# Dilated rows of four streams in one load, a fourth token group's products inside attention, and the next weights converted at its end

## The chip, the cores and the metric

The kernel runs on one core of a Trainium2 chip. The core has a matrix engine (TensorE, PE in the profile), a vector engine (VectorE, DVE), an activation engine (ScalarE, ACT), GpSimd (POOL) and SyncE (SP), which only issues transfers; 16 DMA engines move the data. The metric is the device time of one execution in microseconds, lower is better.

## The reference

Attention over q, k, v of shape (4 batches, 8 heads, 576 positions, 64) in float32, then two gated layers over the 2304 tokens:

```python
rel = pos[:, None] - pos[None, :]
mask_plain = (rel >= 0) & (rel < 32)                        # heads 0 to 3
mask_dil = (rel >= 0) & (rel < 128) & (rel % 4 == 0)        # heads 4 to 7
attn = softmax(where(mask, q @ k.T / 8, -1e9)) @ v
x = attn.transpose(0, 2, 1, 3).reshape(2304, 512)
x = (silu(x @ w_gate) * (x @ w_val)) @ w_out                # 512 -> 1536 -> 512
x = (((x @ w1) * (x @ w2)) @ w3) @ w_out2                   # 512 -> 1024 -> 1024 -> 512
```

The weights come as float64.

## The kernel before

**Attention** is worked through in 18 superblocks `u`, each of 128 query rows: 128 consecutive tokens for the plain heads ("near") and 64 rows of each of two residue streams for the dilated heads ("far"). A dilated head only sees positions of its own residue modulo 4, so each residue is a stream of 144 rows with a plain window of 32. A `part` is one batch and a pair of the four residues; the eight parts lie end to end, 64 rows to a superblock. A far row of a load is thus two streams wide: 128 floats, 512 bytes in one piece. A near row is 64 floats, 256 bytes. Tokens become complete in the order of the parts: the four residues of one batch need two parts, so tokens 0 to 511 are complete after superblock 4, not 3.

The schedule is written out by hand (`manual_schedule`): every engine executes its instructions in program order. The loop is `for u in range(-3, 20)`, and a turn of it is called step `u` here. In step `u` the program has, in this order: loads of q and k for `u+5` (`load_qk`), copies of the transposed probabilities of `u-1` (`t_p_out`), the result of `u-2` as a high part (`x_out_hi`, ScalarE), loads of v for `u+2` (`load_v`), exp of `u+1`, scores and the row maximum of `u+2` (`scores`, `softmax_a`), the low part of the result of `u-2` (`x_out_lo`, VectorE), transposes of q and k of `u+3` (`t_qk`), parts of weight conversions (`part_jobs`), the sums of `u+1` (`softmax_b`) and its division on POOL (`softmax_n`), then transposes of the probabilities of `u` (`t_p`) and the product with v of `u-1` (`av`). Scores are the first thing that PE does in a step, so the start of `sc` on PE marks steps. near and far tiles have three buffers, the v tiles four. SyncE issues all near loads, and the far loads of q and k from superblock 1 on; ScalarE issues the far loads of superblock 0, the far loads of v from superblock 1 on (`vfar`), and the first three weight loads, in halves.

**Weights.** A conversion job turns one 512 KB piece of float64 weights into a high and a low part: five VectorE operations (L115 to L125), a cast on ScalarE (L196), a subtraction on POOL (L197). `part_jobs` runs the jobs `early` (the slice c=0 of w_gate, w_val and w_out) in six parts each: one part a step in steps 1 to 6, two a step in steps 7 to 9, and the last job in steps 17 and 18.

**Filling.** `fill` puts single matmuls of the first layer's up-products (24 for a group of 512 tokens: 12 for the gate, 12 for the value) between attention's, at most four a step until step 15, more in steps 16 to 19. Three of the five token groups are worked off this way. Their results pass through PSUM banks `po3`, `pa` and `pb`; `pa` and `pb` have two buffers each, and attention uses them too. av of the last superblock uses the bank `po2`.

**After attention** PE goes over the slices c (12 of the first layer, 8 of the second) and the five groups: `up_mm`, `up_act`, then `down` of the step before; the products of `down` go through `po0` to `po3` and are added up by VectorE. Conversions of the next slice follow behind `down` (`next_job`).

Of the kernel before, what the change touches and what calls it, by code (L numbers as in the profile page):

```python
# [12 lines left out]
I32 = mybir.dt.int32  # L13
# [10 lines left out]
KW = QB + WINDOW  # L24
NIDLE = 8
SQ = 32
NEG = -1.0e9
# [6 lines left out]
def attention_ffn_kernel(  # L34
# [103 lines left out]

    def job_load_half(job, half):

        _, a, j = job
        if half == 0:
            raw_of[job] = wp.tile([P, 2 * PW], I32, tag="wraw", name=f"raw_w{a}_{j}", bufs=3)
        raw = raw_of[job]
        if j < 2:
            h = slice(half * KT // 2, (half + 1) * KT // 2)
            nc.scalar.dma_start(
                out=raw.rearrange("p (k f) -> p k f", f=2 * P)[:, h],
                in_=words((w_gate, w_val)[j])[:, a * 2 * P:(a + 1) * 2 * P].rearrange("(k p) f -> p k f", p=P)[:, h])
        else:  # L150
            h = slice(half * PW, (half + 1) * PW)
            nc.scalar.dma_start(out=raw[:, h], in_=words(w_out)[a * P:(a + 1) * P, h])

    def job_load(job):
# [46 lines left out]
    def jobs_of(c):  # L201

        res = [[] for _ in groups]
        if c + 1 < NCH:
            first = 1 if c else 2
            if c == NFT - 2:

                res[0].append(("w3", 0, 0))
                res[4].append(("w3", 0, 1))
            if c == NFT - 1:  # L210
                first = 0
            if NFT <= c:
                f = c + 1 - NFT
                res[0].append(("w3", f, 0))
                res[1].append(("w3", f, 1))
                first = 2
            for j in range(3 if c + 1 < NFT else 2):
                res[first + j].append(("w", c + 1, j))
        if 1 <= c <= NJ:
            res[4].append(("wo", c - 1, 0))  # L220
        return res

    early = [("w", c, j) for c in range(1) for j in range(3)]
    jobs += early
    for c in range(NCH):
# [26 lines left out]
    def part_jobs(u):  # L252

        n = len(early)
        for m, at in enumerate((-2, 1, 13)):
            if u in (at, at + 1):
                job_load_half(early[m], u - at)
                jpos[0] = m + 1
        third = PARTS // 3


        upto = max(0, min(u, third) + min(2 * max(u - third, 0), third) + max(0, min(third // 2 * (u - NU + 2), third)))
        while parts[0] < upto:
            next(running)
            parts[0] += 1


# [5 lines left out]


    starts = {}
    for part in range(NU * QB // RES):
        for u in range(NU):
            d = part * RES - u * QB
            if -WINDOW < d < QB:
                starts[u] = d  # L280

    MPER = NB if NB % 2 else NB // 2
    mask = []

    def build_masks():
        gen = att.tile([P, KW], F32, name="m_gen")
        nc.gpsimd.memset(gen, 0.0)
        for h in range(2):
            g = gen[h * QB:(h + 1) * QB, :]

            nc.gpsimd.affine_select(out=g, in_=g, compare_op=ALU.is_ge, fill=NEG,
                                    base=WINDOW, pattern=[[-1, KW]], channel_multiplier=1)
            nc.gpsimd.affine_select(out=g, in_=g, compare_op=ALU.is_ge, fill=NEG,
                                    base=-1, pattern=[[1, KW]], channel_multiplier=-1)
        for u in range(MPER):
            m = att.tile([P, 2, KW], F32, name=f"mask{u}")
            nc.vector.tensor_copy(out=m, in_=gen.rearrange("p (u c) -> p u c", u=1).to_broadcast([P, 2, KW]))
            for h in range(2):
                g = m[h * QB:(h + 1) * QB]
                if (2 * u + h) % NB == 0:  # L300
                    nc.gpsimd.memset(g[:, 0, 0:WINDOW], NEG)
                if u in starts:
                    d = starts[u]
                    if d <= 0:
                        nc.gpsimd.memset(g[:, 1, 0:WINDOW + d], NEG)
                    else:
# [4 lines left out]
            mask.append(m)  # L311

# [11 lines left out]
    RP = DIL // 2  # L324
    near_in, far_in, v_in = {}, {}, {}

    def stream(src, part):

        b, r = divmod(part, RP)
        return src[b, HH:H].rearrange("h (m r) d -> m h (r d)", r=DIL)[:, :, r * 2 * D:(r + 1) * 2 * D]  # L330

    def load_qk(u):
        near = att.tile([P, 2, HH, D], F32, tag="near", name=f"near{u}", bufs=3)
        far = att.tile([P, HH, 2 * D], F32, tag="far", name=f"far{u}", bufs=3)
# [10 lines left out]
        near_in[u], far_in[u] = near, far  # L345

    def load_v(u):
        near = att.tile([KW, 2, HH, D], F32, tag="vnear", name=f"vnear{u}", bufs=4)
        far = att.tile([KW, HH, 2 * D], F32, tag="vfar", name=f"vfar{u}", bufs=4)
# [7 lines left out]
        z = WINDOW if u == 0 else 0  # L357
        if z:
            nc.gpsimd.memset(far[0:z], 0.0)
# [4 lines left out]
        v_in[u] = near, far  # L364

    qkT = {}

    def t_qk(u):
# [5 lines left out]
        if u == 0:  # L374
            nc.vector.memset(kn[:, :, 0:WINDOW], 0.0)
            nc.vector.memset(kf[:, :, 0:WINDOW], 0.0)
        else:
            _, _, kn0, kf0 = qkT[u - 1]
            nc.scalar.copy(out=kn[:, :, 0:WINDOW], in_=kn0[:, :, P:])
            nc.scalar.copy(out=kf[:, :, 0:WINDOW], in_=kf0[:, :, QB:])  # L380
        t = near_in.pop(u)
# [37 lines left out]
    def softmax_a(u, par):  # L419
        if par == 0:  # L420
            sm[u] = att.tile([P, 2, NP, KW], F32, tag="s", name=f"s{u}", bufs=4)
            mx[u] = att.tile([P, 2, NP], F32, tag="mx", name=f"mx{u}", bufs=3)
        m = mask[u % MPER]
        s = sm[u][:, par]
# [44 lines left out]
    def av(u):  # L469
        near, far = v_in.pop(u)  # L470
        far = far.rearrange("k h (r d) -> k h r d", r=2)

# [14 lines left out]
    def x_parts(x, u):  # L487
# [3 lines left out]
        t = t[:, HP:NP, :].rearrange("d p (h q) -> d p h q", h=2)  # L491
        for row, cnt, part, m in runs(u * QB, QB, RES):
            b, r = divmod(part, RP)
            edge = min(max((CUT - b * S) // DIL - m, 0), cnt)
            for a, n in ((0, edge), (edge, cnt - edge)):
                if n:
                    xs = tokens(x, slice(HP, NP), b * S + DIL * (m + a), DIL * n)
                    yield (xs.rearrange("d p (m r) -> d p r m", r=DIL)[:, :, 2 * r:2 * r + 2, :],
                           t[:, :, :, row + a:row + a + n])

# [50 lines left out]
    def filling():  # L551
        for g in range(2):
            for j in range(2):

                pt = bank("po3", f"f{g}_{j}", 1) if (g, j) != (1, 1) else bank("pa", f"f{g}_{j}", 2)
                for n, _ in enumerate(up_product(0, g, j, pt)):
# [5 lines left out]
                    yield  # L562
        pa = bank("pa", "pa0_2", 2)
        pb = bank("pb", "pb0_2", 2)
        upp[0, 2] = pa, pb
        for j, pt in enumerate((pa, pb)):
            yield from up_product(0, 2, j, pt)

# [63 lines left out]
    for u in range(-3, NU + 2):  # L632

        filled[1] = sum(PER for b in range(3) if u > ((b + 1) * RP * RES - 1) // QB + 2)
        quota = 4 if u < NU - 2 else PER
# [6 lines left out]
        attention_end(u)  # L642
    assert filled[0] == 3 * PER

# [109 lines left out]
```

## Time and profile before

| | us |
|---|---|
| median of 3 runs | 892.32 (891.57 to 893.55) |
| the profiled execution | 893.95 |
| its span, first to last instruction | 892.1 |
| PE busy in the span | 868.4 (97%) |
| DVE, ACT, POOL busy | 596.6, 249.1, 305.9 |

The span is what the trace covers; 1.85 us of the profiled execution lie outside it. PE is busy nearly throughout, so what matters is where it stands idle, where it runs at its lower clock, and what it waits for there.

### The profile page before, as it was taken

How to read it: one execution, taken by the hardware profiler on the slowest of the kernel's cores; microseconds unless marked ns; L12 is line 12 of the kernel's file. 1: busy time of each engine (PE TensorE's matmuls, PEld its weight loads, DVE VectorE, ACT ScalarE, POOL GpSimd, SP SyncE). 2: the span in 40 equal slices, each digit the busy share in tenths (PEclk: the TensorE clock that was granted, in tenths of full speed). 3: DMA queues.
4: the chain of work that ended last, by engine and by line, in shares of the span. 5: the costliest groups of instructions: out<-in, count | busy, mean ns of one | idle time of the engine just before them, and what ended most of it. 6: DMA issues, size and time to landing. Idle time of an engine off the chain costs nothing.

```text
span 892.1 us, 13545 instructions
## 1 busy us (share of the span) xinstructions
PE 868.4 (97%) x5192; PEld 726.7 (81%) x5192; DVE 596.6 (67%) x1070; ACT 249.1 (28%) x514; POOL 305.9 (34%) x296
## 2 busy tenths in 40 slices
PE   6898999999999999999999999999999999999998
PEld 4677778888888888888888888888888888888886
DVE  5788766767667676676667784857575747575725
ACT  4778741222212222122221234222121212121211
POOL 5666523323223232232322358423231313231311
PEclk9899999999999999999999999999999999999999
DMA  9877611212112121121211220122121212120014
GB/s 188 187 164 167 155 48 48 70 49 72 48 48 72 48 71 48 48 71 48 71 48 48 71 62 10 41 55 52 43 59 37 63 45 60 47 68 27 1 48 165
DMA packets 113856, 61.77 MB, mean 69 GB/s; under 512 B 72320, under 2 KB 108800, under 8 KB 113792
## 3 DMA queue, kind: packets, MB, share of 16 engines
q1 hardware_dynamic: 104928, 55.73, 23.5%
q10 hardware_dynamic: 8864, 5.18, 2.3%
q8 instruction: 41, 0.67, 0.3%
q14 instruction: 23, 0.19, 0.1%
HBM read 56.16 MB, written 4.72 MB: 68 GB/s over the span
## 4 chain that ended last, share of the span: by engine, by line
PE 90%; DVE 4%; DMA 3%; SPq 1%; issue 0%; ACT 0%; POOL 0%; ACTq 0%; POOLq 0%
PE pa L525 27%; PE pb L525 27%; PE po L670 17%; PE po L690 11%; PE fold L704 5%; PE av L483 1%; DMA far<-in_k_dram 1%; PE pp L459 1%; PE sc L416 1%; PE f L525 1%; DMA vfar<-in_v_dram 1%; DVE x_lo L507 1%; DVE mx L431 1%; DMA vnear<-in_v_dram 1%; DVE s L425 1%; DVE mx L441 0%
## 5 line engine op out<-in xcount | busy, mean ns | idle before, releaser
L582 DVE TENSOR_TENSOR pr<-pb,ga 128x512 f32<-128x512 f32 (+1 forms) x98 | 62.5, 637 | 212.5 <-PE pb L525 108.4
L586 POOL TENSOR_TENSOR sl<-pr,sh 128x512 fp32r<-128x512 f32 (+1 forms) x100 | 118.5, 1185 | 232.7 <-ACT sh L585 232.7
L525 PE MATMUL pa<-x_hi,wlo 128*128 128x512 f32 (+1 forms) x392 | 143.4, 368 | 0.0
L525 PE MATMUL pa<-x_hi,whi 128*128 128x512 f32 (+1 forms) x392 | 143.3, 368 | 0.0
L525 PE MATMUL pb<-x_hi,whi 128*128 128x512 f32 (+1 forms) x392 | 143.3, 368 | 0.0
L525 PE MATMUL pb<-x_hi,wlo 128*128 128x512 f32 (+1 forms) x392 | 143.2, 367 | 0.0
L197 POOL TENSOR_TENSOR wlo<-val_w,whi 128x512 fp32r<-128x512 f32 x52 | 67.2, 1293 | 199.3 <-ACT whi L196 199.3
L656 DVE TENSOR_TENSOR y<-po,y 128x512 f32<-128x512 f32 (+1 forms) x220 | 131.3, 632 | 0.2 <-PE po L670 0.2
L525 PE MATMUL pa<-x_lo,whi 128*128 128x512 f32 (+1 forms) x392 | 128.5, 368 | 0.0
L525 PE MATMUL pb<-x_lo,whi 128*128 128x512 f32 (+1 forms) x392 | 128.4, 368 | 0.0
L585 ACT CAST sh<-pr 128x512 fp32r<-128x512 f32 (+1 forms) x100 | 57.9, 579 | 151.2 <-DVE pr L582 148.5
L196 ACT CAST whi<-val_w 128x512 fp32r<-128x512 f32 x52 | 32.3, 621 | 233.6 <-DVE val_w L125 233.6
L670 PE MATMUL po<-sh,wlo 128*128 128x512 f32 (+1 forms) x240 | 88.4, 368 | 0.6 <-POOL wlo L197 0.6
L670 PE MATMUL po<-sh,whi 128*128 128x512 f32 (+1 forms) x240 | 88.5, 369 | 0.4 <-ACT whi L196 0.4
L670 PE MATMUL po<-sl,whi 128*128 128x512 f32 (+1 forms) x240 | 88.4, 368 | 0.0
L525 PEld LDWEIGHTS pa<-x_hi,wlo 128*128 128x128 f32 x392 | 73.9, 188 | 12.8
L525 PEld LDWEIGHTS pa<-x_hi,whi 128*128 128x128 f32 x392 | 73.9, 188 | 12.7
L525 PEld LDWEIGHTS pb<-x_hi,whi 128*128 128x128 f32 x392 | 73.9, 189 | 12.2
L525 PEld LDWEIGHTS pb<-x_hi,wlo 128*128 128x128 f32 x392 | 73.9, 189 | 12.1
L525 PEld LDWEIGHTS pb<-x_lo,whi 128*128 128x128 f32 x392 | 72.5, 189 | 12.2
L525 PEld LDWEIGHTS pa<-x_lo,whi 128*128 128x128 f32 x392 | 72.4, 188 | 12.3
L656 DVE TENSOR_TENSOR o<-po,o 128x512 f32<-128x512 f32 x126 | 81.4, 685 | 0.2 <-PE po L690 0.2
(100 smaller groups left out, 1345.7 us busy)
## 6 DMA issues: line engine op xcount, KB each, us to landing
raw_w<-in_moe_w_dram SPq DMA_DIRECT2D x256, 32.0 KB, 1.8
raw_w<-in_moe_w_dram SPq DMA_DIRECT2D x16, 512.0 KB, 3.5
raw_w<-in_moe_w_gate_dram SPq DMA_DIRECT2D x11, 512.0 KB, 3.7
raw_w<-in_moe_w_val_dram SPq DMA_DIRECT2D x11, 512.0 KB, 3.6
raw_w<-in_moe_w_out_dram SPq DMA_DIRECT2D x11, 512.0 KB, 3.5
out_dram<-o SPq DMA_DIRECT2D x18, 256.0 KB, 2.1
raw_wo<-in_moe_w_out_dram SPq DMA_DIRECT2D x8, 512.0 KB, 3.4
vnear<-in_v_dram SPq DMA_DIRECT2D x32, 96.0 KB, 4.0
```

The lines of the kernel that those rows point to most:

```text
L196: nc.scalar.copy(out=hi, in_=val)
L197: nc.gpsimd.tensor_tensor(out=lo, in0=val, in1=hi.bitcast(F32), op=ALU.subtract)
L416: nc.tensor.matmul(out=t[rt][x * QB:(x + 1) * QB, p, :], lhsT=lhsT, rhs=rhs, start=True, stop=True)
L425: nc.vector.tensor_tensor(out=s.rearrange("q (t u) c -> q t u c", u=2), in0=sc.pop((u, par)).rearrange("q (t u) c -> q t u c", u=2), in1=m ...
L525: nc.tensor.matmul(out=pt[:, :n], lhsT=a[:, ws], rhs=tokens(x, kk, t0, n), start=i == 0, stop=i == len(terms) - 1)
L582: nc.vector.tensor_tensor(out=pr[:, :n], in0=pb[:, :n], in1=ga[:, :n], op=ALU.mult)
L585: nc.scalar.copy(out=sh[:, :n], in_=pr[:, :n])
L586: nc.gpsimd.tensor_tensor(out=sl[:, :n], in0=pr[:, :n], in1=sh[:, :n].bitcast(F32), op=ALU.subtract)
L656: nc.vector.tensor_tensor(out=dst, in0=src, in1=dst, op=ALU.add)
L670: nc.tensor.matmul(out=po[:, :n], lhsT=a[:, ws], rhs=x[:, :n], start=first, stop=last)
L690: nc.tensor.matmul(out=po, lhsT=x[:, ts], rhs=a[:, ws], start=first, stop=last)
L704: nc.tensor.matmul(out=pt, lhsT=a[:, j % HJ * P:(j % HJ + 1) * P], rhs=b[:, j, :], start=first and j == 0, stop=last and j == NJ - 1)
```

## The change

- Far loads take all four streams of 64 rows at once for two superblocks (`load_far`, `streams`): rows of 256 floats, 1024 bytes in one piece, one tile for a pair with two buffers. The first pair is still loaded by twos (`far0`). The v tiles of the dilated heads are made alike, with two buffers for a pair in place of four for a superblock. Superblock 2p takes streams 0 and 1, superblock 2p+1 streams 2 and 3, so a pair completes 256 consecutive tokens.
- SyncE issues all loads but the first two far ones. `job_load_half` goes; the first three weight pieces are loaded whole, at steps 1, 3 and 11 (before: halves at -2 and -1, 1 and 2, 13 and 14), and converted in steps 3 to 5, 6 to 8 and 14 to 16, two parts a step.
- The masks become ten different ones, picked by what they depend on (before: nine, used cyclically).
- Four groups (`GFILL`) are filled in. The first matmul of a group may come as soon as its 512 tokens are complete, so filling begins at step 6 (before: 7). The main loop computes products from the fifth group on.
- At step 18 (`u == NU`) two whole jobs run at once: w_gate and w_val of slice 1. Before, they ran behind `down` of groups 1 and 2 of slice 0.

```diff
-            first = 1 if c else 2
+            first = 1
...
-            for j in range(3 if c + 1 < NFT else 2):
-                res[first + j].append(("w", c + 1, j))
+            if c == 0:
+                res[4].append(("w", 1, 2))
+            else:
+                for j in range(3 if c + 1 < NFT else 2):
+                    res[first + j].append(("w", c + 1, j))
...
-    jobs += early
+    jobs += early + [("w", 1, 0), ("w", 1, 1)]
...
-        n = len(early)
-        for m, at in enumerate((-2, 1, 13)):
-            if u in (at, at + 1):
-                job_load_half(early[m], u - at)
-                jpos[0] = m + 1
+        for m, at in enumerate((1, 3, 11)):
+            if u == at:
+                load_to(m + 1)
...
-        upto = max(0, min(u, third) + min(2 * max(u - third, 0), third) + max(0, min(third // 2 * (u - NU + 2), third)))
+        upto = sum(min(max(n * (u - at), 0), third) for n, at in ((2, 2), (2, 5), (2, NU - 5)))
         while parts[0] < upto:
             next(running)
             parts[0] += 1
+        if u == NU:
+            next_job()
+            next_job()
...
-        far_queue = nc.scalar if u < 1 else nc.sync
+        near_in[u] = near
+    def load_far(pair, a, n, tag, bufs, queue):
+        far = att.tile([P, HH, n * D], F32, tag=tag, name=f"{tag}{pair}_{a}", bufs=bufs)
         for j, src in enumerate((q, k)):
-            for row, cnt, part, m in runs(u * QB, QB, RES):
+            for row, cnt, b, m in runs(pair * QB, QB, RES):
                 r0 = j * QB + row
-                far_queue.dma_start(out=far[r0:r0 + cnt], in_=stream(src, part)[m:m + cnt])
+                queue.dma_start(out=far[r0:r0 + cnt], in_=streams(src, b)[m:m + cnt, :, a * D:(a + n) * D])
+        for i in range(0, n, RP):
+            far_in[2 * pair + (a + i) // RP] = far[:, :, i * D:(i + RP) * D]
+    def load_qk(u):
+        load_near(u)
+        if u < 2:
+            load_far(0, RP * u, RP, "far0", 2, nc.sync if u else nc.scalar)
+        elif u % 2 == 0:
+            load_far(u // 2, 0, DIL, "far", 2, nc.sync)
...
-        for row, cnt, part, m in runs(u * QB - WINDOW + z, KW - z, RES):
-            queue = nc.scalar if u else nc.sync
-            queue.dma_start(out=far[z + row:z + row + cnt], in_=stream(v, part)[m:m + cnt])
+        if u % 2 == 0:
+            far = att.tile([KW, HH, DIL * D], F32, tag="vfar", name=f"vfar{u}", bufs=2)
...
+            for row, cnt, b, m in runs(u // 2 * QB - WINDOW + z, KW - z, RES):
+                nc.sync.dma_start(out=far[z + row:z + row + cnt], in_=streams(v, b)[m:m + cnt])
...
+        for g in range(2, GFILL):
+            pa = bank("pa", f"pa0_{g}", 2)
+            pb = bank("pb", f"pb0_{g}", 2)
...
-        filled[1] = sum(PER for b in range(3) if u > ((b + 1) * RP * RES - 1) // QB + 2)
+        filled[1] = sum(PER for g in range(GFILL) if u > (groups[g + 1][0] - 1) // P + 2)
...
-            if n > 2:
+            if n >= GFILL:
                 up_mm(c, g)
```

## Rows read from the trace of the kernel before

**Rows 1.** Busy time by window: us, engines (count), granted PE clock, DMA share, GB/s

```profile
0.00:121.45 121.45, 101.41 (x1523) 80.27 (x1523) 89.47 (x199) 84.34 (x217) 72.02 (x105) 0.94 0.74 160
121.45:892.10 770.65, 767.04 (x3670) 646.38 (x3670) 507.09 (x872) 164.78 (x298) 233.86 (x191) 1.00 0.19 55
```

**Rows 2.** The same view, stretches of 10 us, then two stretches of the main part

```profile
10.00:20.00 10.00, 4.67 (x82) 3.65 (x74) 6.18 (x13) 3.61 (x11) 5.90 (x8) 0.96 0.98 196
20.00:30.00 10.00, 9.29 (x132) 8.23 (x134) 6.77 (x16) 7.64 (x21) 6.06 (x8) 0.70 1.00 213
30.00:40.00 10.00, 6.76 (x148) 5.39 (x147) 9.43 (x23) 8.16 (x24) 6.67 (x8) 0.98 0.75 176
40.00:50.00 10.00, 8.94 (x124) 8.08 (x124) 5.31 (x12) 6.24 (x17) 3.64 (x4) 0.68 0.84 191
...
576.00:580.00 4.00, 4.00 (x20) 3.30 (x19) 3.90 (x9) 0.62 (x1) 1.58 (x2) 1.00 0.31 69
...
608.00:612.00 4.00, 4.00 (x20) 3.30 (x19) 3.44 (x7) 1.06 (x2) 2.59 (x2) 1.00 0.34 116
```

**Rows 3.** Chain of waits, 0 to 130 us: start, us, what

```profile
11.42 6.34 DMA vfar<-in_v_dram
17.79 0.33 ACTq L363
...
115.08 1.11 PE av L483 x32
...
126.73 2.72 PE pa L525 x12
```

**Rows 4.** ScalarE in order of time, around 18 us

```profile
18.66 0.84 ACT L437 ACTIVATE s<-s 128x768 f32<-128x768 f32 x1 [4.67 <-DMA near<-in_q_dram]
```

**Rows 5.** PE in order of time: start, us, what [idle before <- releaser]

```profile
20.43 0.92 PE L416 MATMUL sc<-kn,qn 64*64 64x96 f32 x16 [3.86 <-ACT kn L389]
...
45.41 0.92 PE L416 MATMUL sc<-kn,qn 64*64 64x96 f32 x16
...
55.30 0.56 PE L416 MATMUL sc<-kn,qn 64*64 64x96 f32 x16
...
84.51 0.56 PE L416 MATMUL sc<-kn,qn 64*64 64x96 f32 x16
...
89.25 0.56 PE L416 MATMUL sc<-kn,qn 64*64 64x96 f32 x16
...
106.20 0.64 PE L459 MATMUL pp<-ident,s 128*96 128x128 f32 x4 [0.53 <-POOL s L450]
...
120.09 0.50 PE L670 MATMUL po<-sh,whi 128*128 128x512 f32 x1 [0.38 <-ACT whi L196]
...
121.45 0.50 PE L670 MATMUL po<-sh,wlo 128*128 128x512 f32 x1 [0.62 <-POOL wlo L197]
```

**Rows 6.** Transfers of the first 45 us: total, then size and us to landing

```profile
DMA packets 23577, 8.44 MB, mean 188 GB/s; under 512 B 15379, under 2 KB 23571, under 8 KB 23571
...
far<-in_k_dram SPq DMA_DIRECT2D x6, 128.0 KB, 4.1
...
vfar<-in_v_dram SPq DMA_DIRECT2D x1, 128.0 KB, 6.3
```

**Rows 7.** VectorE in order of time

```profile
117.13 0.94 DVE L507 TENSOR_TENSOR x_lo<-av,x_hi 128x256 fp32r<-128x256 f32 x2 [0.92 <-ACT x_hi L503]
...
127.64 0.42 DVE L115 TENSOR_SCALAR val_w<-raw_w 128x512 int32<-128x512 int32 x1
...
129.74 0.69 DVE L125 SCALAR_TENSOR_TENSOR val_w<-raw_w,val_w 128x512 int32<-128x512 int32 x1
```

**Rows 8.** POOL in order of time, its first softmax operation

```profile
9.32 0.83 POOL L432 TENSOR_TENSOR s<-s,mx 128x384 f32<-128x384 f32 x1 [2.58 <-DVE mx L431]
```

**Rows 9.** The page's costliest groups: busy us, mean ns | idle before

```profile
L586 POOL TENSOR_TENSOR sl<-pr,sh 128x512 fp32r<-128x512 f32 (+1 forms) x100 | 118.5, 1185 | 232.7 <-ACT sh L585 232.7
...
L196 ACT CAST whi<-val_w 128x512 fp32r<-128x512 f32 x52 | 32.3, 621 | 233.6 <-DVE val_w L125 233.6
```

More of the change, by code (lines that the diff above doesn't have):

```diff
@@ L25 @@
 NIDLE = 8
+GFILL = 4
 SQ = 32
@@ L136, in slice_tiles @@
         return whl[c]
[L139 to L152, printed above, removed]
     def job_load(job):
@@ L265, in part_jobs @@
             parts[0] += 1
+        if u == NU:
+            next_job()
+            next_job()
     att = tc.alloc_tile_pool(name="att", bufs=1, side="right")
     starts = {}
-    for part in range(NU * QB // RES):
-        for u in range(NU):
-            d = part * RES - u * QB
+    for b in range(B):
+        for pair in range(NU // 2):
+            d = b * RES - pair * QB
             if -WINDOW < d < QB:
-                starts[u] = d
-    MPER = NB if NB % 2 else NB // 2
-    mask = []
+                starts[pair] = d
+    mask, masks = [], {}
     def build_masks():
@@ L294, in build_masks @@
                                     base=-1, pattern=[[1, KW]], channel_multiplier=-1)
[L295 to L304, printed above, removed]
+        for u in range(NU):
+            first = tuple((2 * u + h) % NB == 0 for h in range(2))
+            d = starts.get(u // 2)
+            if (first, d) not in masks:
+                m = att.tile([P, 2, KW], F32, name=f"mask{u}")
+                nc.vector.tensor_copy(out=m, in_=gen.rearrange("p (u c) -> p u c", u=1).to_broadcast([P, 2, KW]))
+                for h in range(2):
+                    g = m[h * QB:(h + 1) * QB]
+                    if first[h]:
+                        nc.gpsimd.memset(g[:, 0, 0:WINDOW], NEG)
+                    if d is not None and d <= 0:
                         nc.gpsimd.memset(g[:, 1, 0:WINDOW + d], NEG)
-                    else:
+                    elif d is not None:
                         w = g[:, 1, 0:WINDOW + d]
@@ L310, in build_masks @@
                                                 pattern=[[0, WINDOW + d]], channel_multiplier=-1)
-            mask.append(m)
+                masks[first, d] = m
+            mask.append(masks[first, d])
     def runs(a, n, size):
@@ L324, in attention_ffn_kernel, with streams, load_near @@
     RP = DIL // 2
[L325 to L332, printed above, removed]
+    near_in, far_in, v_in, v_far = {}, {}, {}, {}
+    def streams(src, b):
+        return src[b, HH:H].rearrange("h (m r) d -> m h (r d)", r=DIL)
+    def load_near(u):
         near = att.tile([P, 2, HH, D], F32, tag="near", name=f"near{u}", bufs=3)
-        far = att.tile([P, HH, 2 * D], F32, tag="far", name=f"far{u}", bufs=3)
         for j, src in enumerate((q, k)):
@@ L356, in load_v @@
             nc.sync.dma_start(out=near[z:KW, h], in_=v[b, 0:HH, m:m + KW - z, :].rearrange("h s d -> s h d"))
-        z = WINDOW if u == 0 else 0
-        if z:
-            nc.gpsimd.memset(far[0:z], 0.0)
-        for row, cnt, part, m in runs(u * QB - WINDOW + z, KW - z, RES):
-            queue = nc.scalar if u else nc.sync
-            queue.dma_start(out=far[z + row:z + row + cnt], in_=stream(v, part)[m:m + cnt])
-        v_in[u] = near, far
+        if u % 2 == 0:
+            far = att.tile([KW, HH, DIL * D], F32, tag="vfar", name=f"vfar{u}", bufs=2)
+            z = WINDOW if u == 0 else 0
+            if z:
+                nc.gpsimd.memset(far[0:z], 0.0)
+            for row, cnt, b, m in runs(u // 2 * QB - WINDOW + z, KW - z, RES):
+                nc.sync.dma_start(out=far[z + row:z + row + cnt], in_=streams(v, b)[m:m + cnt])
+            v_far[u // 2] = far
+        v_in[u] = near
     qkT = {}
@@ L375, in t_qk @@
             nc.vector.memset(kn[:, :, 0:WINDOW], 0.0)
+        else:
+            nc.scalar.copy(out=kn[:, :, 0:WINDOW], in_=qkT[u - 1][2][:, :, P:])
+        if u < 2:
             nc.vector.memset(kf[:, :, 0:WINDOW], 0.0)
         else:
-            _, _, kn0, kf0 = qkT[u - 1]
-            nc.scalar.copy(out=kn[:, :, 0:WINDOW], in_=kn0[:, :, P:])
-            nc.scalar.copy(out=kf[:, :, 0:WINDOW], in_=kf0[:, :, QB:])
+            nc.scalar.copy(out=kf[:, :, 0:WINDOW], in_=qkT[u - 2][3][:, :, QB:])
         t = near_in.pop(u)
@@ L469, in av @@
     def av(u):
-        near, far = v_in.pop(u)
-        far = far.rearrange("k h (r d) -> k h r d", r=2)
+        near, far = v_in.pop(u), v_far[u // 2]
+        far = far[:, :, u % 2 * RP * D:(u % 2 + 1) * RP * D].rearrange("k h (r d) -> k h r d", r=RP)
         t = bank("pb", f"av{u}", 2) if u == NU - 2 else bank("po2", f"av{u}", 1)
@@ L491, in x_parts @@
         t = t[:, HP:NP, :].rearrange("d p (h q) -> d p h q", h=2)
[L492 to L499, printed above, removed]
+        for row, cnt, b, m in runs(u // 2 * QB, QB, RES):
+            xs = tokens(x, slice(HP, NP), b * S + DIL * m, DIL * cnt)
+            yield (xs.rearrange("d p (m r) -> d p r m", r=DIL)[:, :, u % 2 * RP:(u % 2 + 1) * RP, :],
+                   t[:, :, :, row:row + cnt])
     def x_out_hi(u):
@@ L562, in filling @@
                     yield
[L563 to L567, printed above, removed]
+        for g in range(2, GFILL):
+            pa = bank("pa", f"pa0_{g}", 2)
+            pb = bank("pb", f"pb0_{g}", 2)
+            upp[0, g] = pa, pb
+            for j, pt in enumerate((pa, pb)):
+                yield from up_product(0, g, j, pt)
     filler = filling()
@@ L642, in attention_ffn_kernel @@
         attention_end(u)
-    assert filled[0] == 3 * PER
+    fill(PER)
+    assert filled[0] == GFILL * PER, filled
     att.release()
```

4 lines of the change are left out of this document (1 added, 3 removed).

## The prediction

> **What bounds the kernel now.** I read the windows first, cut where `down` of group 0 begins [rows 1]. After 121.45 us PE is busy for 767.04 of 770.65 us: nothing is to be had there but work taken away. Before it 121.45 − 101.41 = 20.0 us are idle, and the clock falls. So the change is decided in attention. Stretches of 10 us [rows 2] show where: PE is busy for 4.67, 9.29, 6.76 and 8.94 us between 10 and 50 us, with the granted clock at 0.70 and 0.68 in two of the four, that is, partly at the lower level of 1.2 GHz. The DMA share there is 0.98, 1.00, 0.75, 0.84: the beginning is short of data, and not only of bandwidth.
>
> The chain of waits says how [rows 3]: a `vfar` transfer issued at 11.42 lands 6.34 us later, at 17.76, and a transfer issue on ScalarE starts at 17.79. The two share no buffer, so an issue also waits for the landing of an earlier transfer. ScalarE stands 4.67 us behind such issues before its next exp, though the wait is put down to a near load [rows 4]; kn comes late, and PE's scores start at 20.43 after 3.86 us idle [rows 5]. A transfer issue in ScalarE's program order thus stalls attention itself.
>
> Steps are read off PE's score groups [rows 5]: step 1 starts at 20.43, step 5 at 45.41, step 7 at 55.30, steps 12 and 13 at 84.51 and 89.25. Four steps of 6.2 us, then two of 4.9, and 4.74 us where PE sets the pace with four fills in it. The end of attention waits for POOL (0.53 us at 106.20) and for w_out: 0.38 and 0.62 us for its high and low part at 120.09 and 121.45.
>
> **Part by part, against the profiled span of 892.1 us.**
>
> *Loads.* By the tiles' shapes, what must have landed before the transposes of superblock 8 (step 5) is 7.5 MB after the change: near 9 × 0.262, five far pairs × 0.524, v 2.0, one weight piece 0.52. Before it is some 7.7 MB. So bytes are not saved. What changes: (a) ScalarE issues nothing after the first two, so the hold of 4.67 us has no place there any more; (b) weights start at step 1 instead of -2; (c) fewer and larger transfers, and far rows of 1024 B. Before, 8.44 MB came in the first 45 us, 188 GB/s [rows 6]; the best 10 us had 213 [rows 2]. In the main part 256-byte rows of w3 move 69 GB/s at a share of 0.31, 223 at full share, and 1024-byte rows of an up-weight 116 at 0.34, 341 [rows 2]. Half the early bytes become 1024-byte rows; the other half at 213 and this half at 341 would give 262 GB/s. I take 213, the nearest measured under load: 7.5 MB in 35.2 us and, with 1.2 us put for what passes before the first bytes move, 36.4.
>
> PE must also keep up. With the hold gone, step 1 starts near 16 (20.43 less 4.4); four steps of 4.74 to 5.4 put step 5 at 35 to 37.6. Superblock 8's transposes follow a step's start by 1.3 us, so data at 36.4 asks for 35.1, and I take 37.0 for PE's pace: 8.4 us earlier than 45.41. Steps 5 and 6 then carry two conversion operations where one stood. One costs (129.74 + 0.69 − 127.64) / 5 = 0.56 us [rows 7], and VectorE, busy for 9.43 of 10 us from 30 on [rows 2], sets the pace there: 1.1 us given back. Term A: **−7.3 us** at step 7. Its bounds: if the four steps keep their 6.2 us and only the hold goes, −4.4 + 1.1 = −3.3; nothing if SyncE inherits the hold; with 262 GB/s and 4.74 us a step (step 5 at 35), −9.3.
>
> The Trainium skill, DMA: Bandwidth & Descriptors, section Specifications, gives 512 B as the least transfer for line rate, so 1024-byte rows would add nothing to 512-byte ones; by it the supply stays at 188 GB/s, the data of superblock 8 are there at 39.9, step 5 starts at 38.6, and the sum of all terms would be 888.5. The main part's rows hint at more, but show no 512-byte rows alone.
>
> Steps 7 to 14 have the same work on each engine; I cost them at nothing. SyncE's own issues fall from 14 to 11 in two steps while one row piece becomes longer; the near and far transfers hide them, with 4.1 us to landing [rows 6] against two steps of lead.
>
> *Masks.* A tenth copy, six more selects and two fills on POOL run before its first softmax operation, which starts after 2.58 us idle [rows 8]: hidden. If not, what exceeds 2.58 us is paid once, under 1 us.
>
> *The fourth group.* 24 matmuls move; twelve take 2.72 us [rows 3], so 5.44 us leave the main part. Four of them land in step 6, where VectorE sets the pace: hidden (0.91 if not). Twenty lengthen steps 16 to 19 at the same price, 4.53 us. Idle time there lies ahead of them in program order, and is not filled by them. Term B: **−0.9** (0 to −0.9).
>
> *w_out converted in steps 14 to 16.* The waits of 0.38 and 0.62 us at the end go [rows 5]. Term C: **−1.0**. In exchange VectorE has 1.1 us more ahead of the sums in steps 14 and 15, and PE already waits for the division that follows (0.53 at 106.20). Term D: **+1.8** (0 to 2.3, twice 1.1 if nothing covers it).
>
> *Two jobs at step 18.* Ten VectorE operations, 5.6 us, stand between x_lo of superblocks 16 and 17, and x_hi of 17 stands behind their casts on ScalarE. Counted from the end of av(16): x_lo(16) is done at 1.9 (0.92 behind x_hi and 0.94 of its own [rows 7]), the jobs at 7.5, the second cast at 8.1 (0.62 [rows 9]), x_hi(17), put as long as x_lo, at 9.0, x_lo(17) at 9.95. PE has 29 fills and av(17) left, 6.6 + 1.1 = 7.7 us [rows 3], then `down` of group 0, whose third bank is `po2`, held by av(17): wanted at 9.0, free at 9.95, so 1.0 us of wait. Next, `down` of groups 0, 1 and 2 now follow without an up-product between 1 and 2. Behind four adds VectorE does the product of group 2 at about 12.7; cast and POOL's 1.19 us [rows 9] give its low part at 15.2, wanted at 14.3: another 1.0. Term E: **+2.0**, from 0 (all under the fills) to 5.6 (nothing covered). What it takes from slice 0, groups 1 and 2, was hidden there: PE is busy without a gap after 121.45.
>
> Sum: −7.3 − 0.9 − 1.0 + 1.8 + 2.0 = −5.4: a span of 886.7. The profiled execution was 893.95, its median 892.32; I take the difference off the median: **886.9 us**.
>
> **Rivals.**
>
> *All covered.* Supply at 262 GB/s, D and E under the fills: −9.3 − 0.9 − 1.0 = −11.2, 881.1. For it: PE's idle time of 20.0 us leaves room. Against: VectorE's 9.43 of 10 us [rows 2].
>
> *Only the hold goes.* The four steps after it keep 6.2 us, A = −3.3: −3.3 − 1.9 + 3.8 = −1.4, 890.9, within what can be told from no change. For it: shares of 0.98 and 1.00 while the bytes stay. The stronger form, SyncE held as ScalarE was, leaves A at 0: 894.2. Against: shares of 0.75 and 0.84 from 30 to 50 us [rows 2], in steps as slow.
>
> *SyncE blocked at vfar (slower).* With two buffers for a pair, the far v load of step u (even) must wait for av(u−1), at the end of that step, and all later loads stand behind it on SyncE: near of u+6, the next far pair, v, a weight piece. The far pair, issued about 3 us after that, is needed two steps and 1.3 us later, 10.8 us at 4.74 us a step. It pays from a landing time of 7.8 us on; the rows show 4.1, at worst 6.3 [rows 6], but of transfers half as large, with less queued at once. At 10 us seven pairs lose 2.2 each, 15.4: 902. It turns the balance from about 8.6 us on (0.77 × 7 = 5.4).
>
> *The change does not do what it says* can hardly be: order and sizes are fixed by the program.
>
> **How the numbers follow.** No-change here means within 0.2%, 890.5 to 894.1; that is about what a measurement of this kernel can tell. Forecast (884 to 890): 0.48. All covered: 0.20. Only the hold goes, or SyncE held: 0.17, most of it within 0.2%. SyncE blocked: 0.11. Step 18 uncovered with the rest as forecast (E at 5.6: 890.5): 0.04. The range 881.0 to 892.5 reaches from the covered case over the one where only the hold goes, and leaves out the blocked one and the ends: about 0.2. Faster: 0.48 + 0.20 and part of the next two, 0.73; within: 0.14; slower: 0.13.
>
> **What the profile after would show.** ScalarE's wait of 4.67 us before an exp gone; scores of step 1 near 16, of step 5 near 37, of step 7 near 48; more GB/s in 10 to 50 us; the granted clock there nearer to 1. VectorE in steps 14 and 15 ahead of POOL and PE's wait before `t_p` of 15 and 16 at 1.5 us or more. No wait for whi or wlo before the first `po`, and instead one for x_lo(17). The prediction is wrong if far or vfar land later than 7.8 us (PE waits for far in odd steps), if clock stretches at half speed turn up elsewhere, or if the stretch from step 7 to 121.45, 66.2 us before, grows by more than the 20 fills and D.

## Result, and the profile after

The changed kernel takes **897.34 us** (median of 6 runs, 896.40 to 898.55), the kernel before 891.82 us beside it (6 runs): a ratio of **1.0061**, 95% interval 1.0048 to 1.0074. It is slower, by little but clear of the interval, and outside the range. The profiled execution has a span of 896.1 us against 892.1.

I read the windows first, attention and its end against the rest, then stretches of 10 us. Columns as in [rows 1] and [rows 2].

```profile
0.00:129.64 129.64, 106.05 (x1544) 83.59 (x1545) 99.17 (x209) 86.04 (x217) 76.21 (x117) 0.95 0.82 160
129.64:896.09 766.45, 762.22 (x3649) 642.15 (x3647) 501.92 (x861) 162.27 (x294) 230.91 (x189) 1.00 0.18 53
...
10.00:20.00 10.00, 6.93 (x122) 4.88 (x114) 8.84 (x20) 7.32 (x21) 7.49 (x10) 1.00 1.02 183
20.00:30.00 10.00, 8.08 (x160) 6.86 (x160) 8.12 (x18) 7.97 (x22) 7.08 (x11) 1.00 1.23 206
30.00:40.00 10.00, 8.56 (x160) 6.73 (x160) 7.91 (x16) 7.30 (x19) 4.65 (x6) 1.00 1.20 206
40.00:50.00 10.00, 6.87 (x108) 5.65 (x110) 9.69 (x22) 6.91 (x22) 7.70 (x9) 1.00 1.10 211
90.00:100.00 10.00, 7.93 (x131) 6.49 (x125) 9.45 (x22) 9.48 (x20) 6.51 (x8) 0.89 0.48 113
100.00:110.00 10.00, 10.00 (x82) 8.04 (x79) 7.19 (x13) 4.53 (x9) 5.93 (x7) 0.76 0.37 125
...
120.00:130.00 10.00, 5.23 (x15) 4.20 (x16) 3.18 (x5) 3.29 (x5) 1.84 (x2) 0.66 0.31 99
```

The beginning is better than in [rows 2]: the clock is full from 10 to 50 us. The end of attention is worse: a clock of 0.89 and 0.76 from 90 to 110 us, and from 120 to 130 us PE is busy for 5.23 us only, at 0.66. PE in order of time says what it waits for; the rows of `sc` open steps 1, 5, 7 and 15, and 138.61 is the first product of the fifth group.

```profile
17.15 0.56 PE L417 MATMUL sc<-kn,qn 64*64 64x96 f32 x16
...
38.38 0.56 PE L417 MATMUL sc<-kn,qn 64*64 64x96 f32 x16
41.57 0.63 PE L394 MATMUL pfar<-ident,far 128*128 128x128 f32 x4 [1.58 <-DMA far<-in_k_dram]
50.73 0.56 PE L417 MATMUL sc<-kn,qn 64*64 64x96 f32 x16
54.28 0.41 PE L394 MATMUL pfar<-ident,far 128*128 128x128 f32 x2 [1.60 <-DMA far<-in_k_dram]
94.23 0.56 PE L417 MATMUL sc<-kn,qn 64*64 64x96 f32 x16
97.19 0.64 PE L460 MATMUL pp<-ident,s 128*96 128x128 f32 x4 [2.07 <-POOL s L451]
...
113.33 0.64 PE L484 MATMUL av<-pT,vfar 96*64 96x64 f32 x16
...
118.73 0.39 PE L522 MATMUL pa<-x_lo,whi 128*128 128x512 f32 x1
124.77 0.80 PE L522 MATMUL pa<-x_lo,whi 128*128 128x512 f32 x1 [5.65 <-DVE x_lo L504]
125.37 0.63 PE L522 MATMUL pb<-x_hi,whi 128*128 128x512 f32 x1
...
129.64 0.39 PE L669 MATMUL po<-sh,whi 128*128 128x512 f32 x1
...
135.97 0.50 PE L669 MATMUL po<-sl,whi 128*128 128x512 f32 x1 [0.51 <-POOL sl L584]
...
138.61 0.28 PE L522 MATMUL pa<-x_hi,whi 128*128 128x256 f32 x1
```

The row of 5.65 us is the largest idle time of the kernel, and no step of the prediction has it. It is a matmul of the fourth group's gate (`pa`), tokens 1536 to 2047, that waits for VectorE's x_lo. The rows of VectorE and ScalarE show which x_lo that is:

```profile
114.94 0.94 DVE L504 TENSOR_TENSOR x_lo<-av,x_hi 128x256 fp32r<-128x256 f32 x2 [4.39 <-ACT x_hi L500]
115.78 0.42 DVE L116 TENSOR_SCALAR val_w<-raw_w 128x512 int32<-128x512 int32 x1
...
119.41 1.44 DVE L120 TENSOR_SCALAR val_w<-val_w 128x512 int32<-128x512 int32 x1
...
121.61 0.69 DVE L126 SCALAR_TENSOR_TENSOR val_w<-raw_w,val_w 128x512 int32<-128x512 int32 x1
123.78 0.94 DVE L504 TENSOR_TENSOR x_lo<-av,x_hi 128x256 fp32r<-128x256 f32 x2 [1.47 <-ACT x_hi L500]
```

```profile
122.34 0.62 ACT L182 CAST whi<-val_w 128x512 fp32r<-128x512 f32 x1 [3.11 <-DVE val_w L126]
122.86 0.88 ACT L500 CAST x_hi<-av 128x256 fp32r<-128x256 f32 x2
```

x_lo of superblock 16 ends at 115.88; ten conversion operations follow; x_hi of 17 stands behind two casts on ScalarE and ends at 123.74; x_lo of 17 ends at 124.72, and PE goes on at 124.77. But superblock 17 writes tokens 2048 to 2303, none of the fourth group's. The two share a tile: x is cut into two, at token 1536 (`CUT`).

The balance, with three rows of the kernel before that were not shown yet:

```profile
99.81 0.56 PE L416 MATMUL sc<-kn,qn 64*64 64x96 f32 x16
...
115.52 0.64 PE L483 MATMUL av<-pT,vfar 96*64 96x64 f32 x16
...
134.73 0.28 PE L525 MATMUL pa<-x_hi,whi 128*128 128x256 f32 x1
```

| stretch | before, us | after, us | difference |
|---|---|---|---|
| 0 to step 7 | 55.30 | 50.73 | −4.6 |
| step 7 to step 15 | 44.51 | 43.50 | −1.0 |
| step 15 to the end of av(16) | 16.35 | 19.74 | +3.4 |
| end of av(16) to the fifth group | 18.57 | 24.64 | +6.1 |
| the rest | 757.4 | 757.5 | +0.1 |

The sum is +4.0, the difference of the spans. In the fourth line 20 fills more (+4.5), 24 matmuls fewer (−5.4) and the two waits for w_out that are gone (−1.0) make −1.9, where the table has +6.1; so new waits cost **8.0**: 5.65 and 0.51 idle, and 1.9 because thirteen matmuls took 4.87 us (124.77 to 129.64) where the price of [rows 3], 0.227 each, gives 2.95; the clock was at 1.2 GHz from 121.8 to 128.6.

### The profile page after: what moved, and what is told of

It is laid out like the page before. It is cut to its first block, busy times and chain, and to the rows that moved or that the text cites. A ratio compares the mean times of both kernels' runs of the same rounds, so it can differ in the third digit from the quotient of the medians.

```text
span 896.1 us, 13488 instructions
## 1 busy us (share of the span) xinstructions
PE 868.3 (97%) x5192; PEld 725.7 (81%) x5192; DVE 601.1 (67%) x1070; ACT 248.3 (28%) x511; POOL 307.1 (34%) x306
## 4 chain that ended last, share of the span: by engine, by line
PE 84%; DVE 1%; issue 1%; POOL 0%; ACT 0%; ACTq 0%
PE pa L522 26%; PE pb L522 26%; PE po L669 16%; PE po L689 11%; PE fold L703 5%; DVE o L655 0%; DVE y L653 0%; POOL sl L584 0%; ACT sh L583 0%; DVE pr L580 0%; ACTq L583 0%
```

## Experiments

My theory after the result: the loss is the shared x tile behind the two jobs; the loads gave what they gave, and the conversion in steps 14 to 16 has its price. The rivals: the waits that the prediction had named (bank `po2`, sl) carry the end; w_out is late rather than dear; and for the missing gain at the beginning, row length or SyncE's hold at `vfar`. Steps are read off `sc` rows throughout. Each ratio is to the kernel before on the same chip.

### The end of attention

**Jobs of slice 1 back behind `down`**, the tile still shared.

```diff
-            first = 1
+            first = 1 if c else 2
...
-    jobs += early + [("w", 1, 0), ("w", 1, 1)]
+    jobs += early
...
-        if u == NU:
-            next_job()
-            next_job()
```

> The two weight jobs of step 18 go back behind down of slice 0, as before the change; all else as in the changed kernel. Theory: x_lo(17) stands behind ten conversion operations, and group 3's products wait 5.65 us for it, 1.8 us more going to the half clock that follows. Then x_lo(17) ends within 2 us of av(17), the wait is under 0.5 us, the clock stays at 1.00 from 120 to 130 us, and the time is 889.5 to 891.5 (up to 1 us lost again in slice 0). Rival, the fourth group itself costs the time (its banks, its place): the wait stays, 896 to 898.

891.91 us, 0.9990 (0.9981 to 0.9999): 5.4 us less than the change, 0.4 above the range expected. With nothing between the two x_lo, the wait shrinks from 5.65 to 1.44 us, though not to the 0.5 expected:

```profile
97.16 1.09 PE L453 MATMUL pp<-ident,s 128*96 128x128 f32 x4 [2.07 <-POOL s L444]
119.55 0.50 PE L515 MATMUL pa<-x_lo,whi 128*128 128x512 f32 x1 [1.44 <-DVE x_lo L497]
128.98 0.50 PE L662 MATMUL po<-sl,whi 128*128 128x512 f32 x1 [0.51 <-POOL sl L577]
136.01 0.50 PE L662 MATMUL po<-sl,whi 128*128 128x512 f32 x1 [0.84 <-POOL sl L577]
```

**A tile of its own for the fifth group**, the jobs staying at step 18.

```diff
-    spans = ((0, CUT), (CUT, NT))
+    LAST = groups[-1][0]
+    spans = ((0, CUT), (CUT, LAST), (LAST, NT))
...
-        i = int(t0 >= CUT)
+        i = int(t0 >= CUT) + int(t0 >= LAST)
```

> The jobs stay at step 18, but the tokens of group 4 get x tiles of their own, so that group 3's products read no tile that superblocks 16 and 17 write. Theory: the 5.65 us wait is one for a tile, not for data; it goes, and what is left is down's wait for bank po2, up to 1.6 us: 890.5 to 892.5. Rival, the conversions are simply uncovered at that place, whoever waits for them: 896 to 898.

890.71 us, 0.9980 (0.9967 to 0.9993): 6.6 us less than the change, by an edit that only changes which tile holds the tokens. The wait of 5.65 us is gone, and now both waits show that the prediction had priced at 1.0 each:

```profile
96.19 0.64 PE L461 MATMUL pp<-ident,s 128*96 128x128 f32 x4 [2.07 <-POOL s L452]
102.06 0.64 PE L461 MATMUL pp<-ident,s 128*96 128x128 f32 x4 [1.77 <-POOL s L452]
...
122.94 0.47 PE L670 MATMUL po<-sh,whi 128*128 128x512 f32 x1 [1.47 <-DVE x_lo L505]
127.99 0.50 PE L670 MATMUL po<-sl,whi 128*128 128x512 f32 x1 [0.50 <-POOL sl L585]
```

1.47 us for x_lo of 17 ahead of the third bank of `down`, and 0.50 for sl. So that mechanism is right, and small; the shared tile stood in front of it.

**w_out earlier still** (loaded at step 7, converted in steps 10 to 12), all else as in the change.

```diff
-        for m, at in enumerate((1, 3, 11)):
+        for m, at in enumerate((1, 3, 7)):
...
-for n, at in ((2, 2), (2, 5), (2, NU - 5)))
+for n, at in ((2, 2), (2, 5), (2, 9)))
```

> w_out of slice 0 is loaded at step 7 and converted in steps 10 to 12 instead of 11 and 14 to 16; the rest as in the changed kernel. Theory: VectorE's conversions ahead of the sums in steps 14 and 15 make PE wait 2.07 us before the transposes of step 15 and bring the half clock of 98 to 105 us: the wait falls to about 0.9 (0.86 before the change), the clock stays at 1.00 there, and 2 to 3.5 us go: 894 to 895.5. Rival, the exp of step 15 is late for the table loads on ScalarE that the earlier filling moved there: the wait stays above 1.8, and the time at 897.

898.05 us, 1.0056 (1.0039 to 1.0073): a miss. The wait of 2.07 us at step 15 fell to 0.80, but step 15 starts at 96.92 instead of 94.23, although step 7 was earlier (49.11 against 50.73): the price moved along with the conversion. The wait behind the shared tile stays, with 5.66 us.

**w_out in steps 17 and 18 again**, with the fifth group's own tile; once with the two jobs at step 18, once with them behind `down`. A third kernel has the jobs behind `down` and w_out in 14 to 16.

```diff
-for n, at in ((2, 2), (2, 5), (2, NU - 5)))
+for n, at in ((2, 2), (2, 5), (3, NU - 2)))
```

> As the run with tiles of its own for group 4, and w_out of slice 0 converted in steps 17 and 18 as before the change (loaded at step 11). Theory: any conversion between steps 10 and 16 costs PE some 3 us since VectorE has none to spare there, and none in steps 17 and 18; but it now stands ahead of x_lo(17) together with the two jobs, so down's wait for po2 grows from 1.47 to about 3 us: 888 to 889.5. Rival, what was lost in steps 15 and 16 comes from elsewhere (table loads of the earlier fill): 890.5 to 892.

> All three edits at the end: tiles of its own for group 4, w_out converted in steps 17 and 18, the two jobs of slice 1 behind down as before the change. The larger loads and the fourth group stay. Theory: the faster start (5.6 us by step 15) is kept, the steps after it last as before plus 20 fills, and no wait for x_lo or w_out is left: 884 to 886.5. Rival, the gain of the start is given back at the next limit whatever stands at the end: 889 to 891.

> The changed kernel with tiles of its own for group 4 and the two jobs back behind down, but w_out converted in steps 14 to 16 as the change has it: the corner that is missing between 890.71 us (own tiles alone) and 888.38 us (own tiles, jobs back, w_out in steps 17 and 18). If the conversion has its price where it stands (from the start of step 15 to the end of av(16) the kernels with it there took 18.8 us, the ones with it in steps 17 and 18 took 16.8), and the end of attention hides it in steps 17 and 18 once the jobs are gone from there, the time is 2.0 us over 888.38: 890 to 891, that is no different from own tiles alone, in which the two jobs then cost the 1.5 us that the wait of 1.47 shows, less what they save later. If the jobs at step 18 are what costs and the conversion is paid back at the end of attention, the time is 888 to 889.

| tile of group 5 | w_out in steps | two jobs | us | step 15 to end of av(16), us |
|---|---|---|---|---|
| shared | 14 to 16 | step 18 | 897.34 | 19.74 |
| shared | 14 to 16 | behind `down` | 891.91 | 18.76 |
| own | 14 to 16 | step 18 | 890.71 | 18.77 |
| own | 14 to 16 | behind `down` | 890.51 (0.9979, 0.9969 to 0.9990) | 18.76 |
| own | 17, 18 | step 18 | 892.28 (0.9999, 0.9984 to 1.0013) | 16.80 |
| own | 17, 18 | behind `down` | **888.38** (0.9943, 0.9921 to 0.9965) | 16.79 |

The kernel with 890.51 us ran on another chip than the other experiments, where the kernel before took 892.10, so its ratio is the one to compare. With the tile cut, the place of the jobs makes no difference that can be told as long as w_out is out of the way (890.71, 890.51). At step 18 they cost the 1.47 us shown above. Behind `down` they cost about as much: from the fifth group's first product to the end the kernels with them there and four groups filled take 758.9 us, the others 757.5, and 0.85 us of it is a wait for sl. The conversion of w_out costs 18.77 − 16.8 = 2.0 us in steps 14 to 16. In steps 17 and 18 it costs nothing if the jobs are not there too: `down` then starts at 117.19 without a wait, since the 20 fills more stand in front of it. With both there, VectorE is late for the bank `po2`, 3.84 us:

```profile
123.94 0.47 PE L670 MATMUL po<-sh,whi 128*128 128x512 f32 x1 [3.84 <-DVE x_lo L505]
```

That kernel is a miss of 3 to 4 us: I had expected that wait, but not the lower clock behind it, 125.4 to 128.8. The last kernel of the table is 2 us slower than expected, and faster than the kernels before and after.

**Three groups instead of four**, on that fastest kernel.

```diff
-GFILL = 4
+GFILL = 3
```

> Built on the kernel with tiles of its own for group 4, w_out in steps 17 and 18 and both jobs back behind down (888.38 us): three token groups' up-products fill attention, as before the change, instead of four. By the prediction's term of 0.9 us for the fourth group (20 of its 24 matmuls lengthen the end of attention at the price that they have later) the time is 889 to 889.7. If the four matmuls of step 6 and waits at the end of attention hide more of them, it is 890 or more; if the fourth group's fills cost more at the end of attention than they save (bank or x tile waits, low clock), it is below 888.

889.40 us, 0.9964 (0.9950 to 0.9977); span 886.0 against 885.0. The time is the one expected, but for another reason, and the single runs overlap (887.78 to 890.93 against 886.84 to 888.95). It doesn't test the term of 0.9 us: filling starts at step 6 in both kernels, so both put four matmuls there, and between the end of av(16) and the fifth group both have 64 matmuls of 128x512. What differs are waits. Without the fourth group's fills the two for w_out are back, 2.2 us:

```profile
113.87 0.50 PE L663 MATMUL po<-sh,whi 128*128 128x512 f32 x1 [1.54 <-ACT whi L183]
...
115.23 0.50 PE L663 MATMUL po<-sh,wlo 128*128 128x512 f32 x1 [0.63 <-POOL wlo L184]
```

Against that, the 0.50 us for sl and the 1.4 us behind `down` are gone. That leaves 0.4 us of the 1.0 between the spans; the other 0.6 are there at the start of step 15, before the edit can matter.

### The beginning

**The far data in more pieces**: first each transfer of q, k and v cut by columns (two transfers of 512-byte rows in place of one of 1024), then cut by rows (the same number of transfers, rows of 1024 bytes). All else as in the change. The edits of v, which are alike, are left out.

```diff
-                queue.dma_start(out=far[r0:r0 + cnt], in_=streams(src, b)[m:m + cnt, :, a * D:(a + n) * D])
+                for i in range(0, n, RP):
+                    queue.dma_start(out=far[r0:r0 + cnt, :, i * D:(i + RP) * D],
+                                    in_=streams(src, b)[m:m + cnt, :, (a + i) * D:(a + i + RP) * D])
...
```

> The far loads of a pair (q, k and v) go out as two transfers of two streams each, rows of 512 bytes instead of 1024; tiles and steps as in the changed kernel. If longer rows and fewer transfers carry the faster start, step 7 starts near 53 instead of 50.73 and the time is 899 to 901. If the start is faster only because ScalarE no longer stands behind issues and weights come later, step 7 starts within 1 us of 50.73: 896.5 to 898.5.

```diff
-                queue.dma_start(out=far[r0:r0 + cnt], in_=streams(src, b)[m:m + cnt, :, a * D:(a + n) * D])
+                for c0, c1 in ((0, cnt // 2), (cnt // 2, cnt)):
+                    queue.dma_start(out=far[r0 + c0:r0 + c1],
+                                    in_=streams(src, b)[m + c0:m + c1, :, a * D:(a + n) * D])
...
```

> The changed kernel with every far transfer cut in two by rows (32 and 32 of 64): rows of 1024 bytes stay, the number of transfers is that of the run with 512-byte rows (902.8, step 7 at 55.97). If the number of transfers carries the start, step 7 starts near 55 and the time is 901 to 904. If the length of the rows does, step 7 starts within 1 us of 50.73: 896.5 to 898.5.

902.82 us, 1.0109 (1.0094 to 1.0124), and 900.44 us, 1.0084 (1.0054 to 1.0113): the first above both ranges expected, the second between the two of its own. Steps 7 and 15 start late in both, first cut by columns, then by rows:

```profile
55.97 0.56 PE L421 MATMUL sc<-kn,qn 64*64 64x96 f32 x16
98.79 0.56 PE L421 MATMUL sc<-kn,qn 64*64 64x96 f32 x16
```

```profile
52.91 0.56 PE L420 MATMUL sc<-kn,qn 64*64 64x96 f32 x16
98.33 0.56 PE L420 MATMUL sc<-kn,qn 64*64 64x96 f32 x16
```

In the change they start at 50.73 and 94.23. So the number of transfers alone, rows kept, costs 2.2 us at step 7 and 4.1 at step 15; the shorter rows add 3.1 at step 7 and 0.5 at step 15. The seven kernels with the change's loads (the change and the experiments above, without the one that loads w_out at step 7) differ among themselves by 2.1 and 2.4 us there (48.60 to 50.73, 92.46 to 94.84), and both new kernels lie outside. The number of transfers is thus shown as a cause. What the length of the rows adds is not settled: 0.5 to 3.1 us by the place where one reads it, 2.4 in the times, whose intervals overlap. The windows of the first kernel show that the DMA engines are not what is full:

```profile
10.00:20.00 10.00, 7.10 (x124) 5.12 (x122) 8.84 (x20) 7.29 (x23) 7.41 (x10) 1.00 0.73 143
20.00:30.00 10.00, 7.96 (x92) 7.08 (x92) 4.32 (x10) 5.47 (x16) 4.87 (x7) 0.66 0.86 191
```

The share is 0.73 and 0.86 (change: 1.02 and 1.23) while PE waits for far data (2.73 us ahead of the transpose at 21.81, with the lower clock from 20.8 to 27.6). The engines have room. What comes late are the issues: SyncE issues the four k transfers of that pair from 18.03 to 19.91, the change its two from 15.96 to 17.03, and each of the pair's smaller transfers lands sooner after its issue, in 2.0 to 2.9 us against 3.2 to 4.5.

**The far v load issued by ScalarE again**, all else as in the change.

```diff
-                nc.sync.dma_start(out=far[z + row:z + row + cnt], in_=streams(v, b)[m:m + cnt])
+                (nc.scalar if u else nc.sync).dma_start(out=far[z + row:z + row + cnt], in_=streams(v, b)[m:m + cnt])
```

> The changed kernel with the far loads of v issued by ScalarE again. If ScalarE's holds behind issues cost the start, holds of some us stand before its exps again, step 7 starts 2 us or more later than 50.73, and the time is 899 to 903. If data supply alone sets the start, step 7 starts within 1 us of 50.73: 896.5 to 898.5.

924.37 us, 1.0347 (1.0327 to 1.0368), 21 us above the slower range expected. ScalarE stands still for 4 to 5 us again and again before an exp, as in [rows 4]; the wait is put down to POOL:

```profile
44.56 0.84 ACT L438 ACTIVATE s<-s 128x768 f32<-128x768 f32 x1 [4.94 <-POOL s L433]
```

What ScalarE stands at is the `vfar` issue in between: by the transfers' rows its issues start at 30.54, 44.10 and 57.36, each 0.03 to 0.04 us after the end of an av, which frees one of the two buffers. So this is the wait for a buffer, another one than the hold of 4.67 us of before, which had four. The run thus says what such a wait costs, and nothing of the hold of before. The next kernel takes ScalarE's issues out of the kernel before.

**Only the queue changed**: the kernel before, with its four buffers and half-size far loads; far v and weight halves issued by SyncE.

```diff
-            queue = nc.scalar if u else nc.sync
+            queue = nc.sync
...
-            nc.scalar.dma_start(
+            nc.sync.dma_start(
```

> The kernel before with nothing changed but the queue: the far v pieces and the weight halves are issued by SyncE instead of ScalarE; sizes, numbers and order of the transfers in the program stay. If ScalarE's hold of 4.67 us is most of the gain at the start, step 1 starts near 16 to 17 instead of 20.43, the first stretch at half clock is gone, step 7 starts at 50 to 52.5 instead of 55.30, and the time is 888 to 890. If the larger transfers carry it, only step 1 is early, the steps behind it stay at 6.2 us or are held by SyncE, step 7 starts at 54 or later, and the time is 891 to 893.

891.52 us, 0.9989 (0.9977 to 1.0000). Neither expectation holds whole:

```profile
16.48 0.56 PE L416 MATMUL sc<-kn,qn 64*64 64x96 f32 x16
...
50.88 0.56 PE L416 MATMUL sc<-kn,qn 64*64 64x96 f32 x16
...
94.50 0.41 PE L393 MATMUL pfar<-ident,far 128*128 128x128 f32 x2 [1.22 <-DMA far<-in_k_dram]
...
97.48 0.56 PE L416 MATMUL sc<-kn,qn 64*64 64x96 f32 x16
```

Step 1 is 4.0 us earlier and step 7 4.4, nearly as much as in the change; but at step 15 only 2.3 are left of it, and PE waits for far data as late as step 14. So taking far v and weight halves off ScalarE, both at once, is most of the gain at step 7. That the change keeps more of it goes with the number of transfers: the three kernels in which SyncE issues 14 loads of q, k and v in two steps start step 15 at 97.48, 98.33 and 98.79, the seven with the change's loads, 11 in two steps, at 92.46 to 94.84. No run has the kernel before with fewer transfers and nothing else changed.

**SyncE's hold at `vfar` taken away**, on the fastest kernel: the pair's far v load is issued one step later, when av(u−1) has ended.

```diff
-        if u % 2 == 0:
+        w = u if u < 3 else u - 1
+        if w % 2 == 0 and w // 2 not in v_far:
...
```

> Built on the kernel with tiles of its own for group 4, w_out in steps 17 and 18 and both jobs back behind down (888.38 us). The far v load of a pair is issued one step later, when av(u-1) has already ended, so that SyncE is not held at it and the loads behind it go out earlier. If SyncE's hold at the two-buffer vfar is what makes the far data of odd steps late (waits of 2.46 us at 40.96 and 1.63 us at 52.18 there), those waits go, step 7 starts 1.5 to 3 us earlier than 48.60, and the time is 885.5 to 887.5. If the supply itself is the limit (the same bytes in the same number of transfers), the waits stay within 0.5 us of theirs, step 7 stays at 48 to 49, and the time is 888 to 889.

887.71 us, 0.9944 (0.9924 to 0.9963), not to be told from 888.38. The waits for far data at 41 and 52 us go, as the theory of the hold has it; others take their place (1.43 us for POOL's s at 41.04), and step 7 starts at 49.29 instead of 48.60, where 1.5 to 3 us less were expected. The hold was real, and taking it away gains nothing.

## Why the prediction was wrong

The sum was −5.4 us; the profiled span moved by +4.0. Of the 9.4 us between them 6.0 lie in term E, 1.7 in A (taken at step 15: −5.6), 1.6 in D.

- **The step that failed is E, "two jobs at step 18", +2.0 us; it cost 8.0.** I followed x_lo of superblock 17 to one reader, `down` through the bank `po2`, "wanted at 9.0, free at 9.95". It has a second one in the tile: "PE has 29 fills and av(17) left" was taken for cover, but the rest of these fills read x_lo of tokens 1536 to 2047, and the tile that holds them also takes the result of superblock 17. With the tile cut the time falls by 6.6 us, with the jobs moved by 5.4; both at once give hardly more (6.8). So it took the shared tile and the jobs together. The waits that E did name measured 1.47 and 0.50 once the tile was cut. E's upper bound of 5.6 was passed as well, since it counted VectorE's operations and not what PE does after the wait. The three filled groups of before end at token 1535, where the tile is cut, and so never met this; the fourth group lies behind the cut.
- **E's second part: the clock.** Behind 5.65 us of idle time thirteen matmuls ran mostly at half speed, 1.9 us. I had priced a wait, not what follows it.
- **A, −7.3, was too large**: −4.6 at step 7 in this execution. Over the seven kernels with these same loads (the change and six of the experiments) step 7 starts at 48.60 to 50.73, 49.5 in the mean, so −5.8. Step 1 (16 predicted, 17.15), step 5 (37.0; 38.38, and 37.6 in the mean of the seven) were near. What was wrong: steps 5 and 6 take 12.35 us, not 11, as PE waits 1.58 us for the far pair in step 5 besides VectorE.
- **A's cause was half right.** The hold on ScalarE was named rightly: without ScalarE's issues step 7 starts 4.4 us earlier. The supply did not rise as the longer rows could have let it: 183 to 211 GB/s in the change from 10 to 50 us, no stretch above the 213 of [rows 2] although half the bytes came in 1024-byte rows. The Trainium skill, DMA: Bandwidth & Descriptors, section Specifications, gives 512 B as the least transfer for line rate. The two kernels that could test it here, with rows of 512 and 1024 bytes in the same number of transfers, leave it open: they differ by 0.5 us at step 15, but by 3.1 at step 7.
- **D, +1.8, was right by mechanism and size**: 2.0 us in three kernels against four. In this execution the stretch grew by 3.4, with the lower clock from 97.9 to 104.7 after the wait of 2.07 us. **C, −1.0, was put down to the wrong edit**: the waits for w_out also go with w_out in steps 17 and 18, because the fourth group's fills stand before `down`. So moving w_out cost 2.0 and gave nothing, unless the two jobs stand at step 18: then it saves 1.6 (890.71 against 892.28).
- **B, −0.9, holds by count only.** Between the end of av(16) and the fifth group there are 64 matmuls of 128x512 instead of 68, 0.9 us at 0.227 each. What the four in step 6 cost there was not measured apart. The masks stayed hidden: POOL's first softmax operation starts at 9.51 instead of 9.32.
- **The rivals.** "SyncE blocked at vfar" needed landings over 7.8 us; the far pairs issued at 21.87 and 45.76 landed in 7.4 to 7.8; PE waited 1.5 to 1.8 us for far data in odd steps, one of the signs named for a wrong prediction, but taking the hold away gave nothing. "Only the hold goes" put −4.4 at step 7, before the conversions; the kernel with only the queue changed has just that, −4.4, and its four steps from 1 to 5 take 6.2 us each in the mean, as the rival has it. By step 15 it has lost half of the gain. Its 891.52 can't be set against the 890.9 of that rival, which holds the terms B to E too.
- **Readings that were off without bearing on the outcome.** `down` of group 0 begins at 120.09 [rows 5], not at 121.45. SyncE issued 12 loads of q, k and v in two steps before, not 14; ScalarE issued the other two. The masks add four fills on POOL, not two.

Open: why SyncE's issues come late when there are more of them. That an issue starts when an earlier transfer lands [rows 3] is seen, but the rule behind it wasn't tried. A far v tile with more buffers, another way to test the hold, wasn't tried either.

## What to carry to other kernels

Before work is pulled forward, list for each tile that it reads all writers of that tile, not only of the part it reads: here the wait was for the tile, and a second cut was worth 6.6 us, more than the gain at the beginning. Price a conversion on VectorE at nearly its full busy time where VectorE sets the pace (here 2.0 us for the 2.2 that stand in steps 14 and 15), and look for the stretch where other work already stands in front of its user. For a beginning that is short of data, count the transfers and look at the engine that issues them, not only at bytes and row lengths.

## What the hardware did that I had not expected

The clock did not follow the same wait in the same way. Behind 2.07 us of idle time in step 15 it was at 1.2 GHz from 97.9 to 104.7 us in the change, from 97.1 to 100.4 in the kernel with only the jobs back, and stayed at 2.4 GHz in the kernel with its tile cut, whose windows there read 1.00:

```profile
90.00:100.00 10.00, 7.93 (x128) 6.47 (x126) 9.73 (x21) 9.63 (x21) 5.99 (x8) 1.00 0.63 162
100.00:110.00 10.00, 8.23 (x71) 6.49 (x70) 6.73 (x12) 3.88 (x8) 5.75 (x6) 1.00 0.20 66
```

The fastest kernel shows no stretch at the lower clock at all, though PE waits there for up to 2.46 us at once. And one VectorE operation, of a kind whose median is 0.43 us, took 1.44 us (119.41), beside a POOL subtraction of the job before it (119.31); in the kernel with its tile cut the same operation took 1.47. No run here shows why.
